# Q, K and V in 64-row tiles whose outputs change row halves midway, computed ahead of gate and up for chunks 1 to 3

## The chip, the cores and the metric

The kernel runs on one core of one Trainium2 chip. The metric is the device time in microseconds (us) of one execution, as the median of several. Five engines work side by side and meet at semaphores: TensorE (PE; its weight loads are shown apart as PEld), VectorE (DVE), ScalarE (ACT), GpSimd (POOL) and SyncE (SP). SP and ACT also issue the transfers (DMA). An engine takes its instructions in the order in which the program queued them, a DMA issue among them. The profile gives the TensorE clock that was granted; it is 1.00 of full speed throughout.

## What is computed

A transformer block's two branches on the same input, 2048 tokens of width D = 576, bf16, added to the input:

```python
xn = _layernorm(x)
q, k, v = split(xn @ wqkv)              # 32 heads of 18
scores = q @ k.T * 18 ** -0.5
mask = (i - j >= 0) & (i - j < 256)     # a sliding window of 256
a = softmax(where(mask, scores, -1e9)) @ v @ wo
h = silu(xn @ w1) * (xn @ w3)           # F = 4608
return x + a + h @ w2
```

## The kernel before

The tokens go in NC = 4 chunks of CH = 512 (TB = 4 tiles of 128). Every operation is put by `add` (L59) into one list; it names what the operation reads (`r`), writes anew (`w`) or goes on writing (`j`), and waits are derived from that. So the order of the calls is the order of each engine's queue.

The contraction over D = 576 is 4.5 times 128 rows. xnT (the normalised input, transposed) holds five slices of 128 rows, [128, 5, 512] for each of two chunks; the last 64 features stand in both halves of the fifth slice (`ln_apply`, L344, writes them twice). xnS holds slices 0 to 3 with the row halves exchanged, made by two DMAs (`xn_swap`, L380).

A chunk c runs in two halves.

**First half (L824 to L884), gate and up.** 36 units of 128 hidden features. `unit_pairs` (L612) issues nine pairs of 64-row matmuls with 512 columns: row half 0 of the array makes one output, row half 1 the other, each in its own PSUM bank, and xnS lets an output keep its row half for all nine slices. ACT makes a tanh (L629), DVE two products (L635, L638) into hT. Between units go the score steps of attention (`scores` L516, `exps` L525 on ACT, `masks` L552 on POOL), placed by a counter `clock` (one count for a pair) between `start` and `last`; the exponentials go to slots: ten of pt, four made of tiles of `stage` ("sh"), four of the tail of hT ("h"). P times V (`pv`, L573) runs for three of four groups of heads here. The layer norm of the next chunk (`ln_stats`, `ln_apply`, `xn_turn` L363) runs here too. w13, the weights of gate and up, have three buffers; they are loaded in halves of 576 KB, one from SP and one from ACT, at every fourth unit (L846).

**Second half (L889 to L923).** `p2_list` (L643) gives 36 x 4 matmuls of w2 with 288 columns for each half of the output width, then five of wo for each token tile, and the output. An item's number is n. w2 comes in 18 loads of 288 KB into four buffers (`load_w2`, L320), each issued from SP where the buffer's last reader has run, 16 matmuls. Two more w13 halves are issued at n = 36 and 70, the fourth P V at n = 19. For c < 3, `proj` slips Q, K and V of the next chunk in: `qk_tile` (L391), nine tiles of five 128-row matmuls with 512 columns, and `v_tile` (L405), four tiles of two times five with 288. Q and K are copied by DVE to `stage` (L403), V to va (L428). `repack` (L448, L470) then moves Q and K of each of eight groups of four heads out of `stage` by DMAs of 18 to 36 rows, here K from ACT and Q from ACT or SP.

**Prologue (L690 to L778).** Chunk 0's layer norm, transposes (`xn_trans`, L357, 128-row, ACT copies at L361), V (`first_v`) and Q, K run before the first unit. There the DVE half of each V copy is held in `moves` until the last tile (L734). Groups 0 and 1 are moved at once, the others during chunk 0's first half, on SP and ACT.

PSUM has eight banks: three pairs in rotation (`job`, L274) and banks 6 and 7 for scores and transposes; the second half uses four as a ring and four as accumulators.

## Time and profile before

| what | us |
|---|---|
| median of 3 runs | 577.41 |
| lowest and highest | 575.61, 577.52 |
| the profiled execution | 574.94 |
| its span, first to last instruction | 573.1 |
| prologue, to the first unit | 23.94 |
| first half of chunk 0 (from unit 0 to the first w2 matmul) | 81.8 |
| second half of chunk 0, with chunk 1's Q, K, V | 56.5 |
| second half of chunk 3, with the last outputs | 44.5 |
| w2 load, issue to landing, median (shortest to longest of 72) | 3.5 (2.9 to 12.7) |
| w13 half, issue to landing, median (shortest to longest of 72) | 7.5 (5.6 to 15.9) |

The page's groups:

```profile
L525 ACT ACTIVATE pt<-ps 128x1024 bf16<-128x1024 f32 (+1 forms) x118 | 119.3, 1011 | 228.5 <-PE ps L516 227.0
L403 DVE CAST stage<-ps 128x512 bf16<-128x512 f32 x36 | 24.6, 687 | 34.3 <-PE ps L399 34.2
L399 PE MATMUL ps<-xnT,wa 128*128 128x512 bf16 x153 | 37.1, 379 | 0.4
```

A line of a group names the source line, the engine, the operation, output and inputs by the program's names, shapes and count; then the time in which one of them ran, the mean of one in ns, and the engine's idle time ahead of them with what ended most of it. Matmuls are pipelined: one is shown with 379 ns, and the next starts 216 ns after it, so a chain of them is counted from start to start. Lines of a chain or a timeline begin with the start and the length in us; "ACTq" and "SPq" are the issue of a DMA by these engines. In a table by stage, each engine's busy time stands with its count in parentheses, in the order PE, PEld, DVE, ACT, POOL, and then the granted clock, the share of the 16 DMA engines and GB/s.

### The profile page before, as it was taken

What the parts mean: (1) busy time and instruction counts of PE and PEld (TensorE: products, weight loads), DVE (VectorE), ACT (ScalarE), POOL (GpSimd) and SP (SyncE); (2) the same over time, 40 slices, a digit from 0 to 9 for tenths busy, and PEclk for the clock granted to TensorE, in tenths of its full rate; (3) what the DMA queues carried; (4) which work ended last, traced back from release to release, by engine and by line L of the source; (5) the groups of instructions that cost most, each with busy time, mean ns of one, the idle gap of its engine ahead of it and who ended that gap; (6) DMA issues with size and microseconds to landing.
All of it is one profiled execution on the core that took longest, in us unless ns stands there. A gap on an engine that the chain in (4) does not pass through costs nothing.

```text
span 573.1 us, 15316 instructions
## 1 busy us (share of the span) xinstructions
PE 565.3 (99%) x6548; PEld 337.8 (59%) x6558; DVE 338.6 (59%) x636; ACT 238.5 (42%) x310; POOL 161.4 (28%) x377
## 2 busy tenths in 40 slices
PE   8999999999999999999999999999999999999998
PEld 4444545667755454566775555546677454555776
DVE  7586887542267787852227777875232577767211
ACT  4156666200047668620005766770000667666000
POOL 6323453400023335440003334443000334443000
PEclk9999999999999999999999999999999999999999
DMA  8989999998627585877762658696666367441552
GB/s 233 190 156 187 177 172 203 203 166 201 147 75 151 113 160 118 167 166 137 182 151 75 166 104 170 123 177 161 128 171 151 81 119 146 120 92 53 134 147 62
DMA packets 118963, 83.60 MB, mean 146 GB/s; under 512 B 25520, under 2 KB 117808, under 8 KB 118896
## 3 DMA queue, kind: packets, MB, share of 16 engines
q1 hardware_dynamic: 82181, 60.16, 48.9%
q10 hardware_dynamic: 36715, 22.47, 19.9%
q8 instruction: 51, 0.84, 0.7%
q14 instruction: 16, 0.13, 0.1%
HBM read 71.07 MB, written 2.36 MB: 128 GB/s over the span
## 4 chain that ended last, share of the span: by engine, by line
PE 91%; DMA 3%; DVE 3%; SPq 1%; issue 1%; ACTq 0%; POOL 0%; ACT 0%
PE ps L621 45%; PE ps L671 24%; PE ps L399 6%; PE ps L516 6%; PE ps L573 4%; PE ps L677 3%; PE ps L413 3%; DMA w<-in_B_w_dram 3%; SPq L470 1%; DVE xn L347 1%; DMA xp<-in_A_x_dram 0%; DVE va L428 0%; PE ps L370 0%; DVE hT L638 0%; DVE gs L635 0%
## 5 line engine op out<-in xcount | busy, mean ns | idle before, releaser
L525 ACT ACTIVATE pt<-ps 128x1024 bf16<-128x1024 f32 (+1 forms) x118 | 119.3, 1011 | 228.5 <-PE ps L516 227.0
L621 PE MATMUL ps<-xnT,w 64*128 64x512 bf16 x1440 | 190.3, 376 | 0.5 <-DMA w<-in_B_w_dram 0.5
L621 PE MATMUL ps<-xnS,w 64*128 64x512 bf16 x1152 | 155.5, 376 | 0.1
L671 PE MATMUL ps<-w,hT 128*128 128x288 bf16 x1152 | 154.8, 286 | 0.1
L552 POOL TENSOR_TENSOR pt<-pt,mk 128x128 int32<-128x128 int32 (+1 forms) x211 | 85.5, 427 | 232.8 <-ACT pt L525 232.6
L635 DVE SCALAR_TENSOR_TENSOR gs<-th,ps 128x512 bf16<-128x512 bf16 x144 | 98.0, 681 | 75.9 <-ACT th L629 74.8
L671 PEld LDWEIGHTS ps<-w,hT 128*128 128x128 bf16 x1152 | 112.0, 98 | 35.7 <-issue 1.9
L621 PEld LDWEIGHTS ps<-xnT,w 64*128 64x128 bf16 x1440 | 67.9, 94 | 60.6 <-issue 1.3
L638 DVE SCALAR_TENSOR_TENSOR hT<-gs,ps 128x512 bf16<-128x512 bf16 x144 | 98.9, 687 | 5.0
L629 ACT ACTIVATE th<-ps 128x512 bf16<-128x512 f32 x144 | 85.5, 594 | 37.7 <-PE ps L621 35.6
L621 PEld LDWEIGHTS ps<-xnS,w 64*128 64x128 bf16 x1152 | 57.4, 94 | 55.4 <-issue 0.4
L516 PE MATMUL ps<-qv,kv 64*128 64x320 bf16 (+2 forms) x720 | 58.5, 252 | 0.2
L516 PEld LDWEIGHTS ps<-qv,kv 64*128 64x128 bf16 x720 | 34.8, 94 | 37.2 <-ACT stage L525 1.5
L684 DVE TENSOR_TENSOR ofin<-ps,xp 128x288 bf16<-128x288 f32 x32 | 14.7, 458 | 68.0 <-PE ps L677 68.0
L403 DVE CAST stage<-ps 128x512 bf16<-128x512 f32 x36 | 24.6, 687 | 34.3 <-PE ps L399 34.2
L428 DVE CAST va<-ps 64x288 bf16<-64x288 f32 x56 | 25.5, 455 | 28.2 <-PE ps L413 27.6
L399 PE MATMUL ps<-xnT,wa 128*128 128x512 bf16 x153 | 37.1, 379 | 0.4
L525 ACT ACTIVATE stage<-ps 128x1024 bf16<-128x1024 f32 x30 | 30.7, 1023 | 13.7 <-PE ps L516 13.5
L595 DVE STREAM_TRANSPOSE od<-oq 128x256 bf16<-128x256 bf16 x64 | 25.8, 427 | 8.2 <-POOL oq L588 5.5
L552 POOL TENSOR_TENSOR stage<-stage,mk 128x128 int32<-128x128 int32 (+1 forms) x54 | 21.8, 425 | 17.3 <-ACT stage L525 17.3
L677 PE MATMUL ps<-wo,oT 128*128 128x288 bf16 x160 | 25.3, 286 | 0.0
L588 POOL TENSOR_TENSOR oq<-uq,rden 128x288 bf16<-128x288 f32 x16 | 10.8, 673 | 51.0 <-DVE rden L587 51.0
(56 smaller groups left out, 270.9 us busy)
## 6 DMA issues: line engine op xcount, KB each, us to landing
w<-in_B_w_dram SPq DMA_DIRECT2D x42, 576.0 KB, 7.6
w<-in_B_w_dram SPq DMA_DIRECT2D x72, 288.0 KB, 3.5
w<-in_B_w_dram ACTq DMA_DIRECT2D x30, 576.0 KB, 6.7
xp<-in_A_x_dram SPq DMA_DIRECT2D x29, 144.0 KB, 8.0
out_dram<-ofin SPq DMA_DIRECT2D x32, 72.0 KB, 1.9
kv<-stage ACTq DMA_DIRECT2D x91, 18.0 KB
oT<-od SPq DMA_DIRECT2D x84, 18.0 KB
xnS<-xnT SPq DMA_DIRECT2D x5, 256.0 KB, 6.2
```

What stands on the lines that cost most here:

```text
L399: add("pe", lambda e, kd=kd, ws=ws: e.matmul(PS[:, b, :], ws, xnT[:, c % 2, kd, :], start=(kd == 0), stop=(kd == 4)), r=["w8" if i == 8 el ...
L428: add("dve", lambda e, dst=dst, src=src: e.tensor_copy(dst, src), r=[("ps", b), ("ps", b + 1)], **kw)
L516: add("pe", lambda e, r0=r0, out_=out_, kb=kb, q0=q0, nb=nb: e.matmul(out_, kv[r0:r0 + 64, g, kb + NV - NB, :], qv[r0:r0 + 64, g, q0 * KB: ...
L525: add("act", lambda e: e.activation(pt_slot(sl)[:, 0:w, :], PS[:, SC[0]:SC[1] + 1, 0:w].rearrange("p r q -> p q r"), ACT.Exp, scale=scale) ...
L552: add("pool", lambda e, vb=vb, mm=mm: e.tensor_tensor(vb, vb, mm, ALU.mult), r=(key if n == 0 else []) + ["mk"], **{"w" if n == 0 else "j" ...
L595: add("dve", lambda e: e.transpose(od[i][:, c0:c0 + CH // 2], oq[:, c0:c0 + CH // 2]), r=["oq", "oq0"], **{"j" if half else "w": [("od", i)]})
L621: add("pe", lambda e, n=n, r0=r0, r=r, k=k, src=src: e.matmul(PS[:, b0 + r, :], w13[sl][r0:r0 + 64, k, fl * 128:(fl + 1) * 128], src, star ...
L629: add("act", lambda e: e.activation(th[i][:], PS[:, bg, :], ACT.Tanh, scale=0.5), r=[("ps", bg)], w=[("th", i)])
L635: add("dve", lambda e: e.scalar_tensor_tensor(out=gs[i][:], in0=th[i][:], scalar=1.0, in1=PS[:, bg, :], op0=ALU.add, op1=ALU.mult), r=[("t ...
L638: add("dve", lambda e: e.scalar_tensor_tensor(out=hT[:, u, :], in0=gs[i][:], scalar=0.5, in1=PS[:, bu, :], op0=ALU.mult, op1=ALU.mult), r= ...
L671: add("pe", lambda e: e.matmul(bank, hT[:, f, tt * 128:(tt + 1) * 128], w2[sl][:, k, :], start=(f == 0), stop=False), r=[("h", f), ("w2", ...
L677: add("pe", lambda e: e.matmul(bank, oT[:, k, tt * 128:(tt + 1) * 128], wo[:, k, d0:d0 + HD], start=False, stop=(k == 4)), r=[("oT", g) fo ...
```

## The change

Q, K and V are computed in 64-row tiles, two outputs at a time. A tile has two parts. In part 0 row half 0 of the array makes output 0 and row half 1 output 1, over five slices (the fifth being the doubled 64 features); in part 1 the outputs have changed row halves, over the four remaining half slices. The first matmuls of part 1 wait for the last ones of part 0. `proj_begin` queues part 0 of a tile, and then part 1 of the tile before it and its copies (`proj_out`). A q tile makes 128 columns of Q and the same of K: DVE copies Q, ACT K. Tile 8 is split by columns, DVE copies. Of a V tile ACT copies one half of the rows, DVE the other, in all chunks.

For chunks 1 to 3 the tiles run at the head of the chunk's first half, in the order of PROJ, instead of in the second half of the chunk before. Groups 0 to 2 are moved there, Q from ACT and K from SP; groups 3 to 7 from SP at units 0, 1, 4, 7 and 8. Score steps start at 44 of a longer clock, and the first four use slots of hT in every chunk. In chunk 0 the tiles stay in the prologue; V's DVE copies are no longer held back, and the transposes are 64-row ones in banks 6 and 7. The last 64 weight rows are loaded twice instead of being padded with zeros.

```diff
-
-        def xn_turn(t, banks):
...
             src = both[:, :, 0:320].rearrange("p r (k f) -> p k r f", f=64)
             dst = xnT[:, c % 2, :, tt * 128:(tt + 1) * 128].rearrange("p k (r f) -> p k r f", f=64)
-            return lambda: add("dve", lambda e: e.tensor_copy(dst, src),
...
+        def proj_part(c, what, banks, part, behind=()):
+
+            kind, i = what
+            last = []
+            for n in range(5 - part):
+                for r in range(2):
+                    x = r ^ part
+                    kd, r0 = (4 if n == 4 else n), 64 * r
+                    rows = slice(r0, r0 + 64)
+                    out_ = PS[:, banks[x], :]
+                    if kind == "q":
+                        c0 = x * D + i * 128
+                        st, mv = wa[rows, kd, c0:c0 + 128], xnT[rows, c % 2, kd, :]
+                        keys = ["wqk"] + xk(c)
+                    elif kind == "8":
+                        out_ = PS[:, banks[x], 0:CH // 2]
+                        st, mv = w8[rows, kd, :], xnT[rows, c % 2, kd, x * (CH // 2):(x + 1) * (CH // 2)]
+                        keys = ["w8"] + xk(c)
+                    else:
+                        out_ = PS[:, banks[x], 0:HD]
+                        c0 = 2 * D + x * HD
+                        st, mv = xnT[rows, c % 2, kd, i * 128:(i + 1) * 128], wa[rows, kd, c0:c0 + HD]
+                        keys = ["wv", ("xnT", c % 2, i)]
+                    first = part == 0 and n == 0
+                    op = add("pe", lambda e, out_=out_, st=st, mv=mv, n=n, r0=r0, first=first: e.matmul(
+                        out_, st, mv, start=first, stop=(part == 1 and n == 3), tile_position=(r0, 0)),
+                        r=keys, after=behind if n == 0 else (), **{"w" if first else "j": [("ps", banks[x])]})
+                    if n == 4:
+                        last.append(op)
+            return last
+
+        def proj_out(c, what, banks):
+            kind, i = what
+            b = banks[0]
+            if kind == "q":
+                add("dve", lambda e: e.tensor_copy(stage[:, i, :], PS[:, b, :]), r=[("ps", b)], w=st_keys(i))
+                add("act", lambda e: e.activation(stage[:, 4 + i, :], PS[:, b + 1, :], ACT.Copy),
+                    r=[("ps", b + 1)], w=st_keys(4 + i))
+            elif kind == "8":
+                add("dve", lambda e: e.tensor_copy(
+                    stage[:, 8, :].rearrange("p (b f) -> p b f", b=2), PS[:, b:b + 2, 0:CH // 2]),
+                    r=[("ps", b), ("ps", b + 1)], w=st_keys(8))
+            else:
+                v_evac(c, i, b, 0, "act")
+                v_evac(c, i, b, 1, "dve")
+
+        COST = {"q": 1.0, "8": 0.5, "v": 0.5625}
+        PROJ = [("q", 0), ("q", 1), ("v", 0), ("q", 2), ("v", 1), ("q", 3), ("v", 2), ("8", 8), ("v", 3)]
+        pend = []
+
+        def proj_end():
+            if pend:
+                c, what, banks, last = pend.pop()
+                proj_part(c, what, banks, 1, last)
+                proj_out(c, what, banks)
+                return what
+
+        def proj_begin(c, what):
+            banks = job()
+            last = proj_part(c, what, banks, 0)
+            got = proj_end()
+            pend.append((c, what, banks, last))
+            return got
...
-        add("sp", lambda e: e.dma_start(wa[0:64, 4, 2 * D:3 * D], A_wqkv[512:576, 2 * D:3 * D]), j=["wv"], dma="wv")
+        for p in range(2):
+            add("sp", lambda e, p=p: e.dma_start(
+                wa[64 * p:64 * p + 64, 4, 2 * D:3 * D], A_wqkv[512:576, 2 * D:3 * D]), j=["wv"], dma="wv")
         add("dve", lambda e: e.memset(oq[:].bitcast(dt.float32), 0.0), w=["oq0"])
-        add("dve", lambda e: e.memset(wa[64:128, 4, :].bitcast(dt.float32), 0.0), w=["wz"])
...
-        add("sp", lambda e: e.dma_start(wa[0:64, 4, 0:2 * D], A_wqkv[512:576, 0:2 * D]), w=["wqk"], dma="wqk")
+        for p in range(2):
+            add("sp", lambda e, p=p: e.dma_start(
+                wa[64 * p:64 * p + 64, 4, 0:2 * D], A_wqkv[512:576, 0:2 * D]), dma="wqk", **{"j" if p else "w": ["wqk"]})
...
         for p in range(2):
             ln_stats(0, xslot[0], p)
-        moves = []
         for i in range(TB):
             if i + 1 < TB:
                 for p in range(2):
                     ln_stats(i + 1, xslot[i + 1], p)
             ln_apply(i, xslot[i])
-            xn_trans(i, ACC[i])
+            xn_turn(i, SC, "act")
             if i == 0:
-                warm(3, 4)
+                warm(3, 3)
             if i == 1:
                 load_w13([("xnT", 0, 1)])
-            if i == TB - 1:
-                for move in moves:
-                    move()
-                moves = []
-            if i:
-                moves.append(first_v(i - 1))
+            proj_end()
+            if i + 1 < TB:
+                proj_begin(0, ("v", i))
...
-        moves.append(first_v(TB - 1))
-        for move in moves:
-            move()
+        proj_begin(0, ("v", TB - 1))
...
-        for _ in qk_atoms(0, issue_first):
-            pass
+        groups = Groups()
+        for what in [("q", 0), ("q", 1), ("q", 2), ("q", 3), ("8", 8), None]:
+            got = proj_begin(0, what) if what else proj_end()
+            for g in groups.got(got):
+                issue_first(0, g)
...
-            start = 20 if c == 0 else 5
+            if c:
+                total += 9 * sum(COST[kind] for kind, _ in PROJ)
+            start = 20 if c == 0 else 44
...
             if c:
-                free += [("sh", n) for n in range(4)]
+                free += [("sh", 0), ("sh", 2)]
...
             def take(n):
-                if n < len(early) and c == 0:
+                if n < len(early):
                     return early[n]
                 return free.pop(0)
...
+            def spaced_step():
+                nonlocal nxt, soon, clock
+                score_step()
+                soon = clock + 7.5
+                room = last - clock - PV_COST * (3 - next_pv) - 5 * sum(v > at_u for v in xt)
+                nxt = max(soon, clock + room / max(1, len(att) - done))
+                clock += 1
+
+            at_u = -1
+            turned = []
+            if c:
+                groups = Groups()
+                for what in PROJ + [None]:
+                    got = proj_begin(c, what) if what else proj_end()
+                    clock += 5 * COST[what[0]] if what else 0
+                    clock += 4 * COST[got[0]] if got else 0
+                    if got:
+                        for g in groups.got(got):
+                            if g < 3:
+                                repack(c, g, "sp", "act")
+                            else:
+                                turned.append(g)
+                    if clock >= nxt:
+                        spaced_step()
+
             for u in range(NF):
+                at_u = u
+                if u in ((0, 1, 4, 7, 8) if c else ()):
+                    repack(c, turned.pop(0), "sp")
...
+                    if c and j == 0:
+                        free.extend([("sh", 1), ("sh", 3)])
...
-            proj = iter([])
+            assert len({*ring_of, *ACC}) == 8
             if c + 1 < NC:
                 for g in range(G):
                     keep_keys(g)
-                proj = (None for gen in (qk_atoms(c + 1, lambda c, g: repack(c, g, "act", ("act", "sp")[g % 2])), v_atoms(c + 1)) for _ in gen)
                 xn_swap(c + 1, ("sp", "act"))
-            proj_at = [36 + 8 * i for i in range(9)] + [116 + 24 * i for i in range(2 * TB)]
...
-                elif n in proj_at:
-                    next(proj, None)
-            for _ in proj:
-                pass
```

## The prediction

> **What bounds the kernel now.** I read the page's busy table and chain first, then the busy times by stage, then the chain in order of time.
>
> ```profile
> PE 565.3 (99%) x6548; PEld 337.8 (59%) x6558; DVE 338.6 (59%) x636; ACT 238.5 (42%) x310; POOL 161.4 (28%) x377
> 247.76:304.50 56.74, 56.58 (x513) 41.52 (x517) 20.66 (x41) 0.60 (x1) 3.31 (x8) 1.00 0.68 155
> 528.67:573.10 44.43, 41.69 (x424) 32.93 (x424) 8.78 (x19) 0.60 (x1) 1.35 (x2) 1.00 0.42 111
> 14.35 9.66 PE ps L399 x44
> 52.12 1.94 PE ps L621 x18
> 532.52 13.83 PE ps L671 x112
> ```
>
> TensorE never rests, at granted clock 1.00. The second line is the MLP's second half of chunk 1, which carries chunk 2's Q, K and V (56.7 us); the third is that of the last chunk, which carries none (TensorE 41.7). Prices from the chain and start to start: a 512-column matmul of 128 rows 0.216 us (L399), a pair of 64-row ones 1.94/9 = 0.216 (L621), a 288-column one 0.1225 (L671; its 0.1235 holds the last drain). So time comes from fewer TensorE columns, and any new wait of TensorE adds in full.
>
> **1. The tiles.** Before, per chunk: 45 matmuls at 0.216 (Q, K) and 40 at 0.1225 (V), 9.72 + 4.90 = 14.62 us. After: four q tiles of 9 pairs at 0.216 (7.78), tile 8 with 9 pairs of 256 columns at half that (0.98), four V tiles of 9 pairs at 0.1225 (4.41): 13.17. Saving 1.45 a chunk, 4.4 for chunks 1 to 3. Weight loads don't bound the narrow pairs: five transpose pairs (L370) at 44.97 are followed by the next unit at 45.11, 28 ns a pair. The wait between halves of a tile is hidden by the next tile's first half (0.55 to 1.08 us against a drain of 0.376 - 0.216 = 0.16); the last tile has 0.43 of cover. Cost nothing; without cover 0.2 each.
>
> **2. The head of chunks 1 to 3.** The banks rotate over three pairs, so the sixth tile (q3) needs the banks of the third (v0), copied out by ACT and DVE. ACT's queue holds, in this order: K of q0, two q moves of group 0, K of q1, five q moves of groups 1 and 2, then v0's half. A move's issue stops ACT:
>
> ```profile
> 30.50 0.40 PE L516 MATMUL ps<-qv,kv 64*128 64x320 bf16 x6
> 30.72 0.61 PE L621 MATMUL ps<-xnT,w 64*128 64x512 bf16 x4
> ```
> ```profile
> 30.28 0.60 ACT L629 ACTIVATE th<-ps 128x512 bf16<-128x512 f32 x1 [0.49 <-PE ps L621]
> 30.29 1.57 ACTq L470 DMA_DIRECT2D qv<-stage  x1
> 31.90 1.02 ACT L525 ACTIVATE hT<-ps 128x1024 bf16<-128x1024 f32 x1 [1.02 <-PE ps L516]
> ```
> ```profile
> 264.44 0.79 ACTq L470 DMA_DIRECT2D qv<-stage  x1
> 265.26 5.55 ACTq L470 DMA_DIRECT2D kv<-stage  x7
> ```
>
> The scores ended at 30.90, the exponential began at 31.90, just behind the issue. A move costs 0.83 with its gap (5.55/7 and 0.03). Counted from the head's start: q0 complete at 3.02 on TensorE, copied by 3.91 (0.2 to see it, DVE's 0.69 of L403); two moves to 5.6; K of q1 (0.6) to 6.2; five moves to 10.4; v0's two copies (0.82, L426) to 11.2. TensorE stands at q3 after 2.16 + 0.86 + 0.61 + 0.86 + 1.08 + 0.49 + 0.61 + 0.86 = 7.55: a wait of 3.7. Bounds: at 0.66 a move (the shortest ACT ones) 2.9; 3.9 if group 1 starts late. I take 3.6, 10.8 for three chunks. The rest has room: v1, q3 and tile 8 are copied before TensorE is back at their banks, two score steps lie inside. The SP moves behind (K of groups 0 to 2, then all of 3 to 7 in units 0 to 8) are about 34 at 0.8 = 27 us, ending before the w13 halves of units 3 and 7 matter (each loads eight units ahead): nothing, and about 1 us a chunk if that cover were gone.
>
> The Trainium skill, "TensorEngine Tiling (Array Packing)", section "PSUM Bottleneck", says that tiling speeds up TensorE but not the emptying of PSUM, which can become the bound, and to use both ACT and DVE for it. By the rule's advice the split would keep pace (wait nothing); the rows of ACT's queue above speak for the wait.
>
> **3. The prologue of chunk 0.** Before, DVE's halves of the V copies were held back until the fourth normalise was queued. Now v0's copy stands ahead of the statistics of tile 3 and the normalise of tile 2:
>
> ```profile
> 7.25 0.59 DVE L347 TENSOR_SCALAR xn<-xp,mv,rstd 128x576 bf16<-128x576 bf16 x2
> 7.75 0.45 DVE L335 BATCH_NORM_STATS2 stats<-xp 128x6 f32<-128x288 bf16 x1
> 8.72 0.61 DVE L347 TENSOR_SCALAR xn<-xp,mv,rstd 128x576 bf16<-128x576 bf16 x2
> 10.55 0.46 DVE L428 CAST va<-ps 64x288 bf16<-64x288 f32 x1
> ```
>
> v0's first half starts at 7.7 (after tile 0's copy), the turn of tile 1 at 8.3, v0 ends at 9.1, its copy (0.93) runs 9.3 to 10.2, statistics and normalise (1.6) to 11.8. Tile 2 is turned at 11.85, not 9.41; v1's copy delays tile 3 to 14.5, not 10.9; all of xnT is there at 15.7, not 12.64. Then v3 (1.1) and 8.76 of Q and K: unit 0 at 25.6 instead of 23.94, +1.7, saving included. q0 is copied at 20.8 where tile 4 was at 17.2, and SP behind it is solid to the w13 half that TensorE met with no slack:
>
> ```profile
> 17.21 0.89 SPq L470 DMA_DIRECT2D qv<-stage  x1
> 28.74 1.37 SPq L310 DMA_DIRECT2D w<-in_B_w_dram  x2
> 41.62 0.67 SPq L310 DMA_DIRECT2D w<-in_B_w_dram  x1
> ```
> ```profile
> 50.21 1.04 PE L621 MATMUL ps<-xnT,w 64*128 64x512 bf16 x8 [0.45 <-DMA w<-in_B_w_dram]
> ```
>
> If all 3.6 passes through, unit 12 is 3.6 late; if that half (8.55 to land) lands as quickly as the quickest (5.6), 1.3. I take 2.7. The two extra loads of weight rows (0.2 MB, about 1 us at the 233 GB/s of that stretch) lie ahead of q and k only; the memset that goes and one warming matmul are worth nothing.
>
> **4. The second half without projections.** It is as short as the last chunk's, but must also take xnS and two w13 halves. In chunk 0 the w2 loads were already just in time:
>
> ```profile
> 126.44 6.27 DMA w<-in_B_w_dram
> 105.80:162.90 57.10, 56.87 (x488) 41.19 (x493) 20.48 (x42) 0.60 (x1) 3.19 (x8) 1.00 0.82 171
> ```
>
> The stage starts at 105.73. The fifth w2 load, issued at 107.89, took 11.0 (landed 118.9), read at 119.3 before; without four projection tiles (4.3) TensorE is there at 105.73 + 64 x 0.1225 + 1.35 (the P V stretch) = 114.9: a wait of 3.9, less the 0.4 of before: 3.5, the low end. Behind it, landings in order were 1.2 to 1.6 apart for a w2 load and 2.7 for a w13 half; two halves and four loads bring the ninth to about 129.5 where 122.8 is needed: 6.7, the high end. I take 5.0. In chunks 1 and 2 the ring is emptier: the second half fill would go at 257.4, land in 7.0 (as the first did), the ninth w2 load 1.2 behind, 265.6 against 264.7 needed: 0.9 each (0 to 2), 1.8.
>
> **5. Scores.** They start at clock 44 instead of 5, but the span they are spread over grows too; the four early slots in hT and two in stage hold 16 steps, the first P V frees more by then. Nothing; a slot missing would cost a wait of about one step (2 us).
>
> **Sum.** -4.4 + 10.8 + 2.7 + 5.0 + 1.8 = +15.9. On the profiled execution (574.94, span 573.1) that gives 590.8; its time lies 2.5 under the median of 577.41, against which I forecast: 593.
>
> **Rivals.**
> - Faster: ACT is done with v0 when TensorE returns, so the columns alone count: four times 1.45, 571.6. It decides where seven issues fit in 7.55 - 3.95 - 0.6 - 0.82 - 0.2 = 2.0 us, 0.28 each; the nearest short issue is the 0.37 of a w2 load, these moves show 0.57 to 0.97. And the prologue and w2 would have to keep their cover. 0.08.
> - The waits cancel the saving: the first stall lets everything else catch up (heads at 0.6 each, w2 as before), 577. 0.04.
> - Low ends all: -4.4 + 8.7 + 1.3 + 3.5 = 9.1, 586. 0.16.
> - The clock falls in the new gaps. The first ten matmuls of the run took 4.45 us, 0.43 each, and four at 6.71 took 0.22 each after 0.7 of idling, the longest gap inside. If 3.7 of idling brings the slow rate back for as long, each gap costs 2.1 more: four gaps, 8.5, 602. No row shows so long a gap. 0.12. The Trainium skill, "TensorE: Matmul & The Clock Gate", section "What's actually happening", has TensorE fall to half rate after one idle window of about 3.4 us; the gaps forecast would only just contain one, which is why I leave it low.
>
> The forecast has 0.60. Low ends, forecast and most of the clock's case give 583 to 602; the forecast's own is 586 to 599. About 0.5% (2.9 us) is what a measurement here can tell. Faster 0.08, same 0.04, slower 0.88.
>
> **What would show it.** Each of three heads has one TensorE gap of 3 to 4 us before q3's first matmul, released by ACT's V copy; if the gap is under 1 us, step 2 is wrong. Tile 2's normalise starts after 11 us, and unit 0 after 25. In chunk 0's second half TensorE waits for a w2 load at its fifth slot; chunks 1 to 3 show 13.2 us of projection matmuls. Wrong altogether if ACT copies v0 ahead of the moves' issue, or w2 lands within 9 us of the stage's start.

## The result, and the profile after

The changed kernel takes 605.54 us (median of 4 runs, 602.51 to 609.67); the kernel before, run beside it, 576.51 (4 runs, 574.36 to 577.52). The ratio is 1.0513 with a 95% interval of 1.0442 to 1.0585: slower by 29 us. The forecast was 593, with a range of 583 to 602. The profiled execution of the changed kernel took 602.51, its span 600.8, at a mean granted clock of 0.986; the longest of its four runs (609.67 us) had the lowest clock, 0.978. The profiled execution is the shortest of the four. Of one experiment below, `e7_after_v`, the ratio rests on two of its four executions, the other two (its profiled one among them) being over 1.5% longer; from its profile only the heads of the chunks are read.

The page of the changed kernel: the busy table, the shares of the chain, and two groups.

```profile
PE 567.5 (94%) x6885; PEld 334.2 (56%) x6885; DVE 316.4 (53%) x595; ACT 254.9 (42%) x350; POOL 161.3 (27%) x377
...
PE 84%; DMA 6%; DVE 3%; ACTq 3%; ACT 1%; issue 1%; SPq 1%; POOL 0%
...
L689 PE MATMUL ps<-w,hT 128*128 128x288 bf16 x1152 | 148.4, 286 | 9.3 <-DMA w<-in_B_w_dram 9.3
...
L404 PE MATMUL ps<-xnT,wa 64*128 64x512 bf16 x288 | 38.1, 406 | 10.1 <-ACT va L451 10.1
```

TensorE is busy for 94% of the span instead of 99%. Two groups hold 19.4 us of its rest: the projection tiles wait 10.1 for ACT's copy of V, and w2 waits 9.3 for its loads. The mean of a projection matmul is 406 ns where the same shape elsewhere has 376: some ran slower.

The stages, cut at the first unit, the first w2 matmul and the last wo matmul of each chunk, in us:

| stage | before | after |
|---|---|---|
| prologue, to unit 0 | 23.94 | 25.97 |
| first halves of chunks 0 to 3, from unit 0 | 81.79, 85.44, 84.26, 84.03 | 83.60, 87.18, 83.73, 82.58 |
| second halves | 55.82, 55.59, 56.21, 41.59 | 44.72, 44.72, 45.59, 41.60 |
| from there to the next unit 0 | 0.71, 0.71, 0.10 | 20.86, 18.81, 18.54 |
| tail | 2.9 | 2.9 |

The last row but one is the head, where Q, K and V now run. The differences sum to 27.7, the difference of the two spans. The table by stage of the changed kernel (stretch, length, busy times of PE, PEld, DVE, ACT, POOL, then the clock, DMA share, GB/s) for the prologue, two second halves, the three heads and the last second half:

```profile
0.00:25.97 25.97, 20.91 (x215) 10.37 (x217) 12.98 (x35) 9.86 (x18) 13.65 (x25) 0.93 0.92 224
154.29:175.15 20.86, 16.98 (x173) 9.37 (x172) 6.49 (x12) 5.88 (x12) 0.74 (x2) 0.84 0.22 49
262.33:307.05 44.72, 41.94 (x426) 32.81 (x424) 8.39 (x18) 0.60 (x1) 3.37 (x8) 1.00 0.72 168
307.05:325.86 18.81, 15.70 (x172) 9.07 (x172) 6.48 (x12) 5.88 (x12) 0.73 (x2) 0.91 0.24 52
409.59:455.18 45.59, 42.12 (x426) 32.77 (x424) 8.39 (x18) 0.60 (x1) 3.38 (x8) 1.00 0.70 162
455.18:473.72 18.54, 15.43 (x173) 8.73 (x173) 6.49 (x12) 5.88 (x12) 0.73 (x2) 0.91 0.25 53
556.30:600.80 44.50, 41.76 (x426) 33.00 (x424) 8.85 (x19) 0.60 (x1) 1.34 (x2) 1.00 0.42 110
```

In a head 3 to 4 us are a gap (length less TensorE's time), and the granted clock is 0.84 to 0.91. In the prologue it is 0.93, at half from 11.74 to 15.15; in the other stages it is 1.00. The last stretch holds 2.9 us of tail, so that a second half without a wait is 41.6; the others are 3.1 and 4.0 longer, all of it TensorE's gaps.

The head of chunk 1, first ACT in the timeline (start, length):

```profile
158.38 1.53 ACTq L495 DMA_DIRECT2D qv<-stage  x2
159.95 0.60 ACT L416 ACTIVATE stage<-ps 128x512 bf16<-128x512 f32 x1 [1.74 <-DVE stage L415]
160.63 4.57 ACTq L495 DMA_DIRECT2D qv<-stage  x5
165.25 0.82 ACT L451 ACTIVATE va<-ps 64x288 bf16<-64x288 f32 x2 [4.71 <-issue]
```

and then TensorE:

```profile
161.11 1.14 PE L404 MATMUL ps<-xnT,wa 64*128 64x512 bf16 x8
166.13 2.32 PE L404 MATMUL ps<-xnT,wa 64*128 64x512 bf16 x10 [3.88 <-ACT va L451]
168.23 2.37 PE L404 MATMUL ps<-wa,xnT 64*128 64x288 bf16 x18
```

Two moves, K of q1, five moves, then v0's copy, and q3's first matmul behind it, after 3.88 us of rest. What follows the rest is slow: nine pairs of 288 columns go from 168.23 to 170.39, 0.24 a pair instead of 0.1225. The same two stretches in the table by stage:

```profile
162.25:166.13 3.88, 0.01 (x2) 0.01 (x2) 0.69 (x1) 0.84 (x3) 0.00 (x0) 0.90 0.24 45
166.13:172.20 6.07, 6.07 (x38) 2.84 (x40) 0.92 (x2) 1.37 (x3) 0.00 (x0) 0.50 0.15 27
```

The clock is 0.50 for 6.07 us behind the gap. In the records it is at half for 6.83 us in this head and for 3.41 in each of the other two.

A second half, that of chunk 1: SP's issues (L310 a w13 half, L327 w2 loads),

```profile
268.27 1.27 SPq L310 DMA_DIRECT2D w<-in_B_w_dram  x1
269.82 2.33 SPq L327 DMA_DIRECT2D w<-in_B_w_dram  x2
272.19 0.63 SPq L310 DMA_DIRECT2D w<-in_B_w_dram  x1
273.74 2.33 SPq L327 DMA_DIRECT2D w<-in_B_w_dram  x2
```

and TensorE's two waits there:

```profile
276.45 4.09 PE L689 MATMUL ps<-w,hT 128*128 128x288 bf16 x32 [0.79 <-DMA w<-in_B_w_dram]
282.54 0.66 PE L689 MATMUL ps<-w,hT 128*128 128x288 bf16 x4 [1.99 <-DMA w<-in_B_w_dram]
```

The w2 load issued at 269.82 landed at 276.41, just behind the half of 268.27 (275.40); the one issued at 273.74 landed at 282.49, just behind the half of 272.19 (281.28). Each wait ends 0.05 after such a landing. Before, with the same loads, projection tiles stood between these matmuls. Chunk 0 waits at the same two places, the first matmuls of the seventh and of the ninth load of the stage:

```profile
123.26 4.17 PE L689 MATMUL ps<-w,hT 128*128 128x288 bf16 x32 [0.66 <-DMA w<-in_B_w_dram]
129.77 0.66 PE L689 MATMUL ps<-w,hT 128*128 128x288 bf16 x4 [2.34 <-DMA w<-in_B_w_dram]
```

The fifth load, issued at 111.74, landed at 116.81, before TensorE came to it at 118.51.

The prologue, DVE and then SP, and TensorE at unit 12:

```profile
9.20 0.94 DVE L453 CAST va<-ps 64x288 bf16<-64x288 f32 x2 [1.35 <-PE ps L404]
10.15 0.46 DVE L335 BATCH_NORM_STATS2 stats<-xp 128x6 f32<-128x288 bf16 x1
...
11.13 0.59 DVE L347 TENSOR_SCALAR xn<-xp,mv,rstd 128x576 bf16<-128x576 bf16 x2
```
```profile
21.19 0.90 SPq L495 DMA_DIRECT2D qv<-stage  x1
...
45.75 0.67 SPq L310 DMA_DIRECT2D w<-in_B_w_dram  x1
```
```profile
54.08 1.04 PE L639 MATMUL ps<-xnT,w 64*128 64x512 bf16 x8 [2.60 <-DMA w<-in_B_w_dram]
```

v0's copy stands ahead of tile 3's statistics, tile 2 is normalised at 11.13 (8.72 before), SP's moves begin at 21.19 (17.21) and the w13 half of unit 12 is issued at 45.75 (41.62). It landed at 54.03, and TensorE had rested 2.60 for it (0.45 before).

Last, two rests in the first half of chunk 1 with no releaser that the profile shows:

```profile
223.07 0.28 PE L591 MATMUL ps<-stage,va 64*20 64x256 bf16 x2 [1.26 <-issue]
...
252.22 0.60 PE L639 MATMUL ps<-xnS,w 64*128 64x512 bf16 x4 [2.11 <-issue]
```

### The profile page after: what moved, and what is told of

Same layout as the page of the kernel before. It is cut to its first block, busy times and chain, and to the rows that moved or that the text cites. A ratio compares the mean times of both kernels' runs of the same rounds, so it can differ in the third digit from the quotient of the medians.

```text
span 600.8 us, 16004 instructions
## 1 busy us (share of the span) xinstructions
PE 567.5 (94%) x6885; PEld 334.2 (56%) x6885; DVE 316.4 (53%) x595; ACT 254.9 (42%) x350; POOL 161.3 (27%) x377
## 4 chain that ended last, share of the span: by engine, by line
PE 84%; DMA 6%; DVE 3%; ACTq 3%; ACT 1%; issue 1%; SPq 1%; POOL 0%
PE ps L639 43%; PE ps L689 21%; PE ps L404 8%; DMA w<-in_B_w_dram 6%; PE ps L534 5%; PE ps L591 3%; PE ps L695 3%; ACTq L495 3%; SPq L495 1%; DVE gs L653 1%; DVE xn L347 1%; DVE hT L656 1%; PE ps L359 1%; DMA xp<-in_A_x_dram 0%; ACT va L451 0%
## 5 line engine op out<-in xcount | busy, mean ns | idle before, releaser
L689 PE MATMUL ps<-w,hT 128*128 128x288 bf16 x1152 | 148.4, 286 | 9.3 <-DMA w<-in_B_w_dram 9.3
L543 ACT ACTIVATE pt<-ps 128x1024 bf16<-128x1024 f32 (+1 forms) x112 | 113.1, 1010 | 66.6 <-PE ps L534 66.2
L570 POOL TENSOR_TENSOR pt<-pt,mk 128x128 int32<-128x128 int32 (+1 forms) x199 | 80.1, 424 | 87.2 <-ACT pt L543 87.0
L647 ACT ACTIVATE th<-ps 128x512 bf16<-128x512 f32 x144 | 85.5, 594 | 26.3 <-PE ps L639 25.6
L416 ACT ACTIVATE stage<-ps 128x512 bf16<-128x512 f32 x16 | 9.6, 597 | 157.1 <-PE ps L404 151.8
L570 POOL TENSOR_TENSOR hT<-hT,mk 128x128 int32<-128x128 int32 (+1 forms) x31 | 12.4, 421 | 187.4 <-ACT hT L543 187.4
L404 PE MATMUL ps<-xnT,wa 64*128 64x512 bf16 x288 | 38.1, 406 | 10.1 <-ACT va L451 10.1
L543 ACT ACTIVATE stage<-ps 128x1024 bf16<-128x1024 f32 x24 | 24.6, 1023 | 14.1 <-PE ps L534 13.8
L404 PEld LDWEIGHTS ps<-xnT,wa 64*128 64x128 bf16 x288 | 15.1, 99 | 26.9 <-ACT va L451 11.6
L453 DVE CAST va<-ps 64x288 bf16<-64x288 f32 x32 | 14.7, 460 | 26.5 <-PE ps L404 26.2
L404 PE MATMUL ps<-wa,xnT 64*128 64x288 bf16 x288 | 25.4, 316 | 0.7 <-ACT xnT L366 0.5
```

The lines of the kernel that those rows point to most:

```text
L404: op = add("pe", lambda e, out_=out_, st=st, mv=mv, n=n, r0=r0, first=first: e.matmul(out_, st, mv, start=first, stop=(part == 1 and n == ...
L543: add("act", lambda e: e.activation(pt_slot(sl)[:, 0:w, :], PS[:, SC[0]:SC[1] + 1, 0:w].rearrange("p r q -> p q r"), ACT.Exp, scale=scale) ...
L570: add("pool", lambda e, vb=vb, mm=mm: e.tensor_tensor(vb, vb, mm, ALU.mult), r=(key if n == 0 else []) + ["mk"], **{"w" if n == 0 else "j" ...
L647: add("act", lambda e: e.activation(th[i][:], PS[:, bg, :], ACT.Tanh, scale=0.5), r=[("ps", bg)], w=[("th", i)])
L689: add("pe", lambda e: e.matmul(bank, hT[:, f, tt * 128:(tt + 1) * 128], w2[sl][:, k, :], start=(f == 0), stop=False), r=[("h", f), ("w2", ...
```

## The experiments

The theory after the result: the 11.8 us beyond the sum (27.7 of span against 15.9) are three things. The half clock behind the heads' gaps, w13 halves in front of w2 loads in all three second halves, and the later chain of SP in chunk 0. The rivals: that 64-row tiles cost more than their columns wherever they stand; that transfers in general no longer keep up; and, for the prologue, that chunk 0 is held by something other than the V copies. Each kernel is the changed one with the edit shown; ratios are to the kernel before, run beside it.

**e1_moves_sp**: the heads' Q moves from SP instead of ACT.

```diff
-                                repack(c, g, "sp", "act")
+                                repack(c, g, "sp")
```

> Edit to the changed kernel: at the head of chunks 1 to 3 the seven Q moves of groups 0 to 2 go out from SP instead of ACT. Theory (ACT's issues stand ahead of V's copy, and the gap they make lets the clock fall): the three TensorE gaps of 3.88, 3.11 and 3.11 us and the three stretches at half clock (6.8, 3.4, 3.4 us long) go; heads of about 14.5 us instead of 20.9, 18.8, 18.5, the span 600.8 falls by 14 to 16 to about 586. Rival (the copies by ACT and DVE are too slow for three bank pairs, whoever issues): gaps of 2 to 4 us stay at the same place, the span stays within 4 us. Second rival (SP gets too late with group 0, a score step waits): the gap moves to the first score step of the head, 1 to 4 us.

Measured: 597.48, ratio 1.0396 (1.0354 to 1.0438). The heads take 13.71, 14.17 and 13.71 without half clock: 16.6 us less in sum, the gap and the clock both gone. But the first halves are longer by 2.3, 2.0, 4.0 and 1.7; the first of these is chunk 0's, which the edit doesn't touch (see e2). SP in the first half of chunk 1, then DVE, then TensorE:

```profile
183.48 0.48 SPq L296 DMA_DIRECT2D xp<-in_A_x_dram  x1
184.01 0.79 SPq L495 DMA_DIRECT2D qv<-stage  x1
```
```profile
187.18 0.46 DVE L335 BATCH_NORM_STATS2 stats<-xp 128x6 f32<-128x288 bf16 x1 [3.93 <-DMA xp<-in_A_x_dram]
```
```profile
189.66 0.39 PE L639 MATMUL ps<-xnT,w 64*128 64x512 bf16 x2 [2.00 <-DVE hT L656]
```

SP issues moves without a pause until about 208, and other transfers wait in its queue among them. A load of the next chunk's input goes out at 183.48 instead of 175.55. DVE waits for it, its products behind are late, and TensorE rests 2.00 for one of them (0.81 in the same way in chunk 2). w13 halves that are late in the same queue cost 0.80, 1.01 and 1.44 in chunks 1 to 3. What follows: ACT's queue is what held TensorE, and the moves put on SP are not free there; of 16.6 us won only 5.5 reach the end of the span (595.3).

**e2_five_moves**: ACT issues five moves ahead of v0's copy instead of seven.

```diff
-                                repack(c, g, "sp", "act")
+                                repack(c, g, "sp", "act" if g < 2 else None)
```

> Edit to the changed kernel: of the seven Q moves that ACT issues at the head, only the two of group 2 go to SP; five stay. Theory (0.8 us of gap for each move): the three gaps shrink by 1.6 to about 1.5 to 2.3 us. The clock: if it needs an idle stretch of about 3.4 us, no stretch at half clock is left after the heads, and the span falls by 3 x 1.6 + 6.8 = 11 to 12; if shorter gaps are enough, the half-clock stretches stay and the span falls by 5.

Measured: 599.30, ratio 1.0394 (1.0358 to 1.0430). Heads of 15.46 each, gaps of 1.43 each, no half clock. Two moves fewer take 1.68 from the wait of 3.11: 0.84 a move, as priced. The half clock in the heads is gone with 1.43 of rest. The second half of chunk 0 is 49.9 here, with one rest of 3.62 and a half clock of 6.8 behind it. That is not the edit, which begins with chunk 1: chunk 0's instructions are the same in the changed kernel, e1, e2 and e6, and still its second half took 44.72, 44.32, 49.90 and 48.89, and chunk 0 ended at 154.29, 156.57, 160.81 and 158.67. So a difference of a few us in chunk 0 between two profiles says little about an edit, and the changed kernel's profile is the shortest of the four there.

**e3_w13_act**: the second half's two w13 halves from ACT.

```diff
                 if n in (36, 70):
-                    load_w13_half()
+                    load_w13_half((), "act")
```

> Edit to the changed kernel: the two w13 halves that are loaded in each second half (n = 36 and 70) are issued by ACT instead of SP, so they are in another ring than the w2 loads; behind ACT's o_pack issues they also go out some 6 to 10 us later. Theory (w2 loads wait behind the halves in SP's ring): the waits of the second halves of chunks 0 to 2, 3.1, 3.1 and 4.0 us, fall under 0.5 each, the span by 9 to 10. Rival (the DMA engines are full whoever issues): half of the waits or more stay, the span falls by 0 to 5.

Measured: 595.65, ratio 1.0336 (1.0303 to 1.0368). The second halves of chunks 0 to 2, in the table by stage:

```profile
110.37:155.02 44.65, 41.62 (x402) 32.54 (x400) 8.29 (x18) 0.60 (x1) 3.28 (x8) 1.00 0.79 184
260.64:303.58 42.94, 41.83 (x426) 32.84 (x424) 8.39 (x18) 0.60 (x1) 3.38 (x8) 1.00 0.73 175
407.21:448.84 41.63, 41.63 (x426) 32.91 (x424) 8.39 (x18) 0.60 (x1) 3.39 (x8) 1.00 0.74 177
```

Chunk 2's wait is gone (4.0 to 0.0), chunk 1's is 1.3 instead of 3.1, chunk 0's stays at 3.0. The same bytes are moved in less time (177 GB/s against 162 in chunk 2), so the waits come from when and where the halves are issued, not from the amount; in chunk 0 that isn't enough. The edit changes both: from ACT, the halves of chunk 1 go out 14.0 us into the second half (274.66) instead of 5.9 (268.27 in the changed kernel). And SP's w2 loads beside them still land late: the one issued at 275.97 landed at 285.33, 9.4 later, and TensorE waited 1.11 for it. So a w2 load can be late beside halves from another queue too, and this run doesn't separate the queue from the time.

**e5_w13_late**: the two halves at n = 150 and 200, still from SP.

```diff
-                if n in (36, 70):
+                if n in (150, 200):
```

> Edit to the changed kernel: the two w13 halves of each second half stay on SP but are issued at n = 150 and 200 instead of 36 and 70, behind the stretch in which TensorE waited. Theory (w2 loads wait behind a half in their ring): the waits of the second halves of chunks 1 and 2 (3.1 and 4.0 us) fall under 0.5 unless they come back behind n = 150, where a half of 7 us stands in front of w2 loads that have 6 us of lead (then 1 to 2 us there); chunk 0 keeps what its full DMA queues cost, which issuing from ACT left at 3.0: if it falls under 1 here, it was the halves, if it stays at 3, the backlog of the first half. Span lower by 4 to 10.

Measured: 597.31, ratio 1.0369 (1.0321 to 1.0417). Chunk 0's second half is 41.50, with no wait; chunk 1's is 43.86, and chunk 2's 45.78, with rests of 0.72 and 1.19 in the one and 2.42 and a half clock in the other, all behind n = 150. The wait moves with the halves: each time it is for a w2 load issued behind one.

**e4_v_held**: DVE's copies of V in the prologue held back until the last tile, as before the change.

```diff
-                v_evac(c, i, b, 1, "dve")
+                if hold is None:
+                    v_evac(c, i, b, 1, "dve")
+                else:
+                    hold.append(lambda: v_evac(c, i, b, 1, "dve"))
...
+            if i == 0:
+                hold = []
+            if i == TB - 1:
+                held_v, hold = hold, None
+                for move in held_v:
+                    move()
```

> Edit to the changed kernel: in the prologue the DVE copies of V tiles 0 and 1 are held back until tile 3's normalise is queued, as before the change. Theory (the copies ahead of the statistics delay tiles 2 and 3, and SP behind them the w13 half of unit 12): unit 0 starts at 23 to 23.5 instead of 25.97, the gap of 2.6 us at 51.5 shrinks to about 0.5, the span falls by 3 to 4.5. Rival (only the start of unit 0 matters, the w13 half is late for its own reasons): unit 0 as said, but the gap at unit 12 grows to 4 and the span falls by under 1.5.

Measured: 599.81, ratio 1.0440 (1.0387 to 1.0493). Unit 0 begins at 22.59, 3.4 earlier. The rest of chunk 0, SP and then TensorE:

```profile
43.25 0.67 SPq L310 DMA_DIRECT2D w<-in_B_w_dram  x1
```
```profile
53.79 1.89 PE L644 MATMUL ps<-xnT,w 64*128 64x512 bf16 x8 [4.60 <-DMA w<-in_B_w_dram]
```

The half of unit 12 is issued 2.5 earlier, takes 10.5 to land (53.74), and TensorE waits for it at the same place as in the changed kernel, now 4.60. In and behind that rest the clock is at half, from 52.45 to 59.28; the stretch behind it in the table by stage:

```profile
53.79:59.28 5.49, 5.49 (x28) 2.05 (x30) 0.31 (x1) 1.51 (x2) 0.73 (x2) 0.50 0.96 169
```

The first half of chunk 0 grows to 89.35. The held copies explain the late unit 0 (2.9 of the 3.4: e6, which has the changed kernel's prologue and no half clock in it, begins unit 0 at 25.46). In this execution nothing of that reaches the end (span 603.8). But the profile is of the longest of four executions, where the changed kernel's is of the shortest, and the ratio of 1.0440 against 1.0513 leaves room for some 4 us, with overlapping intervals: how much the prologue's time is worth is not decided.

**e8_prologue**: e4's edit, and the first w13 halves of units 3 and 7 of chunk 0 from ACT, past SP's moves.

```diff
-                    load_w13((), "act")
+                    load_w13((), "act", "act" if c == 0 and u < 8 else "sp")
```

> Edit to the changed kernel: V's DVE copies in the prologue held back as in the run before, and in chunk 0 the w13 halves of units 3 and 7 that SP issued behind its moves are issued by ACT. Theory (the first unit is on time with the copies held back, and then SP's queue of moves makes the half for unit 12 late): unit 0 at 22.6, the gap of 4.6 us ahead of unit 12 falls under 1, chunk 0's second half starts at about 106 to 107 instead of 109.6, the span falls by 3 to 5. Rival (the DMA engines are full in chunk 0, whoever issues): the half lands no earlier, the gap of 4 to 5 us stays or comes at unit 16, the span falls by under 1.

Measured: 602.07, ratio 1.0438 (1.0402 to 1.0474). Unit 0 at 22.78, no gap at unit 12, w2 begins at 106.69, 2.9 earlier than in the changed kernel. The second half that follows:

```profile
106.69:155.33 48.64, 43.72 (x402) 32.94 (x400) 8.30 (x18) 0.60 (x1) 3.29 (x8) 0.96 0.81 168
```

It takes 48.64 instead of 44.72: rests of 0.43, 0.92, 2.64 and 0.87 for w2, and a stretch at half clock (0.96 is the mean). In this execution all that was won is given back. But here too the profile is of the longest of four, 48.64 lies within what chunk 0's second half takes without an edit to chunk 0 (44.3 to 49.9, see e2), and the ratio of 1.0438 against 1.0513 again leaves room for some 4 us with overlapping intervals: the run doesn't decide either.

**e6_filler**: twelve pairs of 64-row matmuls of 512 columns ahead of q3 in each head, 2.6 us of TensorE whose results are not used. They fill the gap and change nothing on ACT.

```diff
+                    if what == ("q", 3):
+                        for n in range(12):
+                            for r in range(2):
+                                add("pe", lambda e, r=r: e.matmul(
+                                    PS[:, SC[r], :], wa[64 * r:64 * r + 64, 0, 0:128], xnT[64 * r:64 * r + 64, c % 2, 0, :],
+                                    start=True, stop=True, tile_position=(64 * r, 0)),
+                                    r=["wqk"] + xk(c), **{"j" if n else "w": [("ps", SC[r])]})
```

> Edit to the changed kernel: twelve pairs of 64-row matmuls (2.6 us) into banks 6 and 7, whose results nobody uses, are queued ahead of q3 in the heads of chunks 1 to 3, where TensorE waited 3.1 to 3.9 us for ACT. Theory (the idle stretch lets the clock fall, and that is paid on top of the wait): q3 starts when it did, 11.2 to 11.7 us into the head, but no half-clock stretch follows; the span falls by 3 to 7 (half of 6.8 + 3.4 + 3.4 us of half clock). Rival (the half clock after the heads is unrelated to the gap, or costs nothing since ACT sets the pace): half-clock stretches stay or the span stays within 1.5; with the matmuls not fitting it grows.

Measured: 607.19, ratio 1.0537 (1.0502 to 1.0573). The head of chunk 1:

```profile
158.70:175.75 17.05, 16.59 (x197) 10.63 (x196) 6.48 (x12) 5.88 (x12) 0.74 (x2) 1.00 0.25 56
```

The heads take 17.08, 17.14 and 17.14, at clock 1.00, with gaps of 0.46 to 0.53: 6.9 us less in sum than in the changed kernel (20.86, 18.81, 18.54), with 7.8 us of extra work in them and the same wait for ACT. That is the price of the half clock, measured by itself. The whole run is no faster: chunk 0's second half, which the edit doesn't touch, took 48.89 (w2 waits of 6.1), and the first halves of chunks 1 and 2 have rests marked "issue" of 4.4 and 4.0, for which see the last section.

**e7_after_v**: ACT issues one Q move of groups 1 and 2 behind q2's copy and one each in units 0, 1, 3 and 4, so that V's copies go first.

```diff
                         for g in groups.got(got):
-                            if g < 3:
+                            if g == 0:
                                 repack(c, g, "sp", "act")
+                            elif g < 3:
+                                for key, issue in keyed_moves(c, g, "sp", "act"):
+                                    if key[0] == "q":
+                                        q_later.append(issue)
+                                    else:
+                                        issue()
...
+                    if got == ("q", 2):
+                        q_later.pop(0)()
...
+                if c and u in (0, 1, 3, 4):
+                    q_later.pop(0)()
```

> Edit to the changed kernel: ACT still issues all seven Q moves of groups 0 to 2 in chunks 1 to 3, but the five of groups 1 and 2 stand behind V's and q2's copies in its queue: one after q2, one each in units 0, 1, 3 and 4. Theory (the place in ACT's queue is the fault, not the number of moves nor the engine): the three gaps fall under 0.5, heads of 13.7 to 14.2 us, no half clock after them, and the first halves stay as with the changed kernel (87.2, 83.7, 82.6), where giving all seven to SP made them 89.2, 87.7, 84.3; the span falls by 14 to 17. Rival (ACT has no room in the units either): heads as said, first halves 2 to 4 us longer.

Measured: ratio 1.0188 (1.0140 to 1.0237), from 588.89 and 585.97. A head:

```profile
160.90:174.60 13.70, 13.70 (x173) 9.48 (x172) 6.38 (x12) 5.78 (x12) 0.73 (x2) 1.00 0.25 54
```

All three take 13.74, and TensorE never rests in them. ACT and DVE together empty PSUM in time when only the two moves of group 0 stand ahead of v0's copy: the wait was the order on ACT, and not the work of copying.

**e9_in_place**: the 64-row tiles alone, in the second half of the chunk before, as ten blocks between w2 matmuls; copies by DVE, scores and slots as before, prologue as in e8.

```diff
+            proj = iter([("q", 0), ("q", 1), ("q", 2), ("q", 3), ("8", 8)] + [("v", i) for i in range(4)] + [None] if c + 1 < NC else [])
+            proj_at = (36, 52, 68, 84, 102, 124, 148, 172, 196, 212)
...
+                elif n in proj_at and c + 1 < NC:
+                    what = next(proj)
+                    got = proj_begin(c + 1, what, (ring(), ring())) if what else proj_end()
+                    for g in groups.got(got) if got else ():
+                        repack(c + 1, g, "act", ("act", "sp")[g % 2])
```

> One part of the change alone: the 64-row tiles whose outputs change row halves, but where the old tiles were, in the second half of the chunk before (ten blocks, both copies by DVE, moves from ACT and SP as before the change); the prologue as in the last experiment on it, scores and slots as before the change. Theory (the tiles do save columns, the losses all come from the move): no gaps at heads, no w2 waits over 0.5, no half clock; against the kernel before, chunk 0 about 1 us longer, each second half 1.45 shorter less what 20 changes between 128-row and 64-row matmuls cost (about 0.1 each by the 2.55 us in which twenty w2 matmuls ahead of the P V stretch were followed by it, where 2.45 are columns): -0.4 to +0.6 a chunk, the time within 0.5% of the kernel before. Rival (the tiles themselves are slow between w2 matmuls): second halves 2 us longer or more, the time over 1% longer.

Measured: 579.61, ratio 1.0082 (1.0065 to 1.0100). Its profile has no wait for w2 and records no change of the clock (two of the other five executions have a mean clock of 0.997). Yet the second halves, counted to the next unit 0 since V's last tile stood there before, are 56.79, 56.98 and 56.99 where they were 56.53, 56.30 and 56.31: 0.5 longer on average, not 1.45 shorter. TensorE at two blocks:

```profile
111.23 1.25 PE L404 MATMUL ps<-xnT,wa 64*128 64x512 bf16 x10
112.41 2.13 PE L698 MATMUL ps<-w,hT 128*128 128x288 bf16 x16
114.48 2.12 PE L404 MATMUL ps<-xnT,wa 64*128 64x512 bf16 x18
```

Five pairs take 1.18 to the next block, not 5 x 0.216 = 1.08, and sixteen w2 matmuls 2.07, not 16 x 0.1225 = 1.96. So 0.1 is lost at each change between 64-row and 128-row matmuls; twenty changes a chunk are about 2.2 us, against the 2.0 between the two. The first halves are 1.0, 0.6, 0.0 and 1.3 longer than before the change, with rests of 1.45 for a Q move, 1.35 ("issue") and 1.81 for DVE in chunks 0, 1 and 3. The first rival has its point, but only for tiles set among 128-row matmuls; in a head they stand in one piece ahead of 64-row units.

**e10_repaired**: the move kept, with the repairs of e7, e8 and the w13 halves from ACT at n = 150 and 200.

```diff
-                if n in (36, 70):
-                    load_w13_half()
+                if n in (150, 200):
+                    load_w13_half((), "act")
```

> The move kept and all its waits repaired at once: Q moves of groups 1 and 2 behind V's copies on ACT, the two w13 halves of the second half from ACT at n = 150 and 200, V's copies of the prologue held back, and the w13 halves of units 3 and 7 of chunk 0 from ACT. Theory (the losses are these waits and the half clock that they bring): heads 13.7, second halves 41.6 to 42.5 in chunks 1 and 2, chunk 0's under 44; span 573 to 579. Rival (chunk 0 is bound by its transfers, so what is saved in its first half comes back as waits in its second): chunk 0's second half 46 to 49 again, span 580 to 586.

Measured: 577.01 (12 runs) against 575.44, ratio 1.0028 (1.0010 to 1.0045). A head and a second half:

```profile
153.03:166.89 13.86, 13.86 (x173) 9.48 (x173) 6.38 (x12) 5.78 (x12) 0.74 (x2) 1.00 0.25 54
252.79:295.11 42.32, 41.85 (x426) 32.83 (x424) 8.39 (x18) 0.60 (x1) 3.39 (x8) 1.00 0.72 177
```

With the order on ACT and SP repaired, nearly all of the 29 us is gone, though the tiles and their place are those of the change. Second halves of 42.79, 42.32 and 42.31 are 0.7 to 1.2 above 41.6, with w2 waits of 0.9, 0.5 and 0.5. The profile has one window at half clock, from 58.39 to 61.80, behind a rest marked "issue" of 2.17. Of the twelve executions the six with a mean clock of 1.00 took 574.94 to 577.11, the six with 0.996 or 0.997 took 576.90 to 580.12.

**e11_tuned**: e10, with chunk 0's score steps from 27 on, the two w13 halves at n = 250 and 290, and the loads of x spread over units 26 to 32.

```diff
-            start = 20 if c == 0 else 44
+            start = 27 if c == 0 else 44
...
-                if n in (36, 70):
-                    load_w13_half()
+                if n in (250, 290):
+                    load_w13_half((), "act")
```

> The repaired kernel with three more shifts against waits that its trace still shows: chunk 0's first score step at clock 27 instead of 20 (it waited 1.13 us for a K move), the two w13 halves of the second half at n = 250 and 290 (w2 waits of 0.71, 0.47 and 0.54), and the four input loads of unit 29 spread over units 26 to 32. Theory (these waits are all that is left besides TensorE's waits for its own instructions): 2.5 to 3 us less, a median of 574 to 575, 0.1 to 0.4% under the kernel before, which this measurement can hardly tell from the same. Rival (chunk 0's transfers set its pace, and waits only move): the same median as the repaired kernel, 577, within 0.6.

Measured: 575.91 (12 runs) against 575.88, ratio 1.0012 (0.9989 to 1.0035): no difference. Two second halves, of chunks 0 and 2:

```profile
104.53:149.14 44.61, 41.78 (x402) 32.53 (x400) 8.28 (x18) 0.60 (x1) 3.26 (x8) 1.00 0.81 187
390.46:432.19 41.73, 41.73 (x426) 32.92 (x424) 8.38 (x18) 0.60 (x1) 3.37 (x8) 1.00 0.76 183
```

The columns are saved (4.4) and unit 0 is 1.35 earlier than before the change (22.59), but chunk 0's second half is still 3.0 above 41.6 (w2 waits of 2.6), chunk 1's 0.9 (0.7), and the first halves hold two "issue" rests of 1.80 and 1.43. No version beat the kernel before.

## Why the prediction was right and where it was wrong

The sum against the profiles, in us:

| term | forecast | measured | how |
|---|---|---|---|
| columns | -4.4 | -4.4 | 44.34 in the second halves above 41.6 and in the hand-overs before; 3 x 13.31 in the heads after, without the two score steps (0.43) |
| heads' wait for ACT | +10.8 | +10.1 | gaps of 3.88, 3.11, 3.11 |
| half clock in the heads | 0 | +6.9 | heads 58.21, less 3 x 13.74, less the gaps; e6 agrees |
| w2 waits | +6.8 | +10.2 | 3.1, 3.1, 4.0 |
| prologue and first halves | +2.7 | +4.9 | 2.0 + 2.9, score steps moved to the heads counted back; about 0.5 of the 2.0 is half clock in the prologue |
| sum | +15.9 | +27.7 | |

These are the profile's figures; between the medians it is +29.0.

**Right.** The tiles: TensorE takes what the columns say. The head: q3 waits for the third tile's banks behind seven issues, as step 2 had it, and each of the three gaps has the releaser and the place that were named. e2 gives 0.84 a move, e7 shows that with five of the seven behind the copies nothing is waited for; so the row decided. (The low bound of step 2 is miscounted: seven moves at 0.66 leave a wait of about 2.5, not 2.9. The range hardly moves by it.) The advice of the Trainium skill, "TensorEngine Tiling (Array Packing)", section "PSUM Bottleneck", to split the copies between ACT and DVE, is enough in e7 and not in the changed kernel: it holds as long as few issues stand ahead of a copy (two in e7; five in e2 leave 1.43 of wait). Step 3, link by link: tile 2's normalise at 11.13 (11.8 forecast), unit 0 at 25.97 (25.6; 25.46 in e6, without the half clock from 11.74), the half of unit 12 issued 4.1 late, and unit 12 begun 3.9 late (54.08 against 50.21), a little over the high bound of 3.6.

**Wrong; the clock, the w2 waits of chunks 1 and 2 and the first halves put the time above the range.**

The clock. It stood as a rival at 0.12, "The clock falls in the new gaps", priced at 2.1 a gap and four gaps. Its mechanism came true in all three heads, at 3.2, 2.0 and 1.7 (and in the prologue, at about 0.5), and was left out of the sum for a wrong reason: that the gaps "would only just contain" a whole idle window. The records show that no whole window is needed. In the changed kernel the granted clock changes only at multiples of 3.413 us from one another; in the twelve traces of this case that record changes of the clock (e9's has none), from 20 us on and up to the last whole window but one, each of the 26 such windows at full clock in which TensorE rested for 62% or more was followed by one at half clock, as were 2 of 5 with 57 and 58%, and none with 56% or less. In the e1 run, a rest of 2.04 us at 276.98, in a window that rested 64% in all, brought half clock from 280.4; in the changed kernel 2.60 at 51.47, split over two, brought none. A gap of 3.11 leaves 2.12 (62%) in one window unless its first part is between 0.99 and 2.12 long, which is one position in three; a gap of 1.43 (e2) never does by itself. The Trainium skill, "TensorE: Matmul & The Clock Gate", section "What's actually happening", has the window, that it runs free of the kernel, and half rate after an idle window: the 3.413 us and the clock of 0.50 agree, but "idle" has to be read as mostly idle, which is what the forecast missed.

The second halves of chunks 1 and 2. Step 4 put "0.9 each", taking that a second half fill lands in 7.0 and the ninth w2 load 1.2 behind. It took 9.1 (272.19 to 281.28), since the first half, issued 3.9 earlier, landed only at 275.40; so the ninth load came at 282.49. The first half made a wait of its own ahead of that (0.79). 3.1 and 4.0 in place of 0.9 each: the term was mis-sized by 5.3. e3 and e5 show the mechanism, a w2 load that is issued while w13 halves are under way: the wait shrinks or goes when they are issued later from ACT, and comes back where they are issued later from SP. Whether it takes the same queue is open, since in e3 loads from the other queue were late too. "In chunks 1 and 2 the ring is emptier" was not a reason, since two halves alone fill it.

Chunk 0's second half. The sum's 5.0 (bounds 3.5 to 6.7) met 3.1, by another way than the low bound's. That bound has the fifth load land 11.0 after its issue; it landed after 5.1, 7.2 after the stage's start, and TensorE didn't wait at the fifth slot. The forecast had named that wait as its sign, and a landing within 9 as a sign against it. The waits are those of the high bound, behind the w13 halves. That the size is near is luck as well: with the same instructions chunk 0's second half was 8.3 above 41.6 in e2 and 7.3 in e6.

Chunk 1's first half. TensorE's rests marked "issue" took 3.4 in it, where the whole profile before has 1.04 (0.73 and 0.31). No step foresaw them, and their cause is not shown by an experiment.

Whether prologue and w2 are independent, as the sum took for granted, is open. The profiles of e4 and e8 win 3.4 and 3.2 us at unit 0 and none at the end, where a half or a w2 load that lands at its own time takes up what TensorE gains; the ratios of all their executions leave room for some 4 us kept. The rivals on the fast side ("ACT is done with v0 when TensorE returns", "the first stall lets everything else catch up") are excluded by the heads' gaps.

What stays open besides: why the w13 half of unit 12 takes 8.3 us to land in the changed kernel and 10.5 in e4, and what makes chunk 0's second half vary from 44.3 to 49.9 among executions of the same instructions.

## What to carry to other kernels

Matmuls that are moved out of a stage were also its cover: before moving them, list each load that was just in time there, and what stands ahead of it in its queue. A copy that frees a PSUM bank must not be queued behind DMA issues, at 0.8 us each on an engine that is otherwise idle; and a rest of TensorE of 2 to 4 us should be counted with the half clock behind it, about 1.7 us (half of it) for each window of 3.4. Saving 4.4 us of columns was worth nothing here even with all of that repaired (e11: 1.0012, 0.9989 to 1.0035).

## What the runs showed of the hardware

**The clock** falls after a window of 3.413 us in which TensorE rests for about 60%, in the windows counted above. It comes back only after a window with little rest: of the windows at half clock, the 28 with 22% of rest or less were followed by full clock, the five with 23 to 39% by another at half. That is why the head of chunk 1 lost two windows: its gap of 3.88 reached 0.8 into the window from 165.3, which was already slow.

**A change between 64-row and 128-row matmuls** costs TensorE about 0.1 us (e9, two rows: 1.18 against 1.08, 2.07 against 1.96). The Trainium skill, "TensorEngine Tiling (Array Packing)", section "Key Properties", says that changing the tiling mode drains TensorE; the rows fit that, and give a size, which the page doesn't.

**TensorE's own instructions.** The rests with "issue" as their end come in all thirteen traces, 0.25 to 2.88 us long, mostly in or just behind P V, where many short matmuls follow one another. One transfer lies ahead of each. The DMA view of the changed kernel from 218 to 224 us has it (queue, kind: packets, MB, share):

```profile
q8 instruction: 1, 0.02, 1.2%
```

It began at 220.6 and took 1.1; TensorE's rest ended at 223.07, 1.36 later. Of 34 such rests in the thirteen traces, 33 ended 1.24 to 1.63 us after such a transfer's end, one 2.04; most of these transfers (54 in the changed kernel, with two rests) are followed by none. That speaks for TensorE waiting for its next instructions, and would make a kernel with more matmuls in short bursts pay for it (6,885 here against 6,548 before); no experiment tested it, so it stays a reading of the trace.
